# mLSTM layer and two-matrix MLP on one core: the MLP takes 256 tokens at a time, and the first chunk's second matrix is used in float32 before it is divided

## The chip, the cores and the metric

The kernel runs on one NeuronCore of one Trainium2 chip. The metric is the device time of one execution in microseconds (us); several runs are summed up by their median. Engines are called as in the profile: PE (matmul), PEld (the loading of PE's weights), DVE (elementwise and PSUM reads), ACT (activation functions), POOL, and SP, which issues the DMAs here. Every engine works through its own queue in program order and waits on semaphores for the others.

## The reference: what is computed

A gated linear attention over 4 batches, 8 heads and 768 tokens with heads of 40, and behind it a two-matrix MLP over all 3072 tokens, all in float32:

```
for t in range(768):                       # per batch and head
    m_new  = max(f[t] + m, i[t])
    f_s, i_s = exp(f[t] + m - m_new), exp(i[t] - m_new);  m = m_new
    C = f_s * C + i_s * outer(v[t], k[t]);  n = f_s * n + i_s * k[t]
    y[t] = sigmoid(o[t]) * (C @ q[t]) / max(abs(n @ q[t]), 1)
x = y.transpose to (3072, 320)
h = x @ w_in                               # (320, 2048)
out = (h * erf(softplus(h))) @ w_out       # (2048, 320)
```

## The kernel before

**Work.** The 768 tokens of a batch go in six chunks of 128 (`NC = 6`). One *step* is one chunk of one batch: scores of the 8 heads (L454), a decay matrix `dm` times the scores (L463), the product with the values and with the carried state (L482, L486), the state's update (`pk`, L497, L503, L515), the denominators (L522 to L525), the gate (L530, L535), and three transposes into `pt` (L542, L544), from which ACT writes the rounded half `xh` (L551) and DVE the remainder `xl` (L555). Six chunks times four batches make 24 steps.

The MLP follows chunk by chunk, 8 *units* per chunk, 48 in all. The matmuls round their operands (type fp32r), so that each float32 product is made of three: high by high, low by high, high by low. A unit has two `up` tiles (L691, eight matmuls per 128 columns of `w_in`; the last 64 rows of `w_in` are stacked, high over low), which ACT copies to `hb` (L699). ACT then makes softplus (L703) and erf (L708), each for a batch of units, since each needs another function table (L769); DVE multiplies (L713), rounds to `gh` (L717) and subtracts to `gl` (L721). The `down` matmuls take `gh` with `woh` (L740), `gh` with `wol` (L741) and `gl` with `woh` (L738), 320 columns each, into four PSUM tiles `po0` to `po3`, one per batch. ACT copies them to `o`, and a DMA writes them out. In chunk 0 a unit is 256 tokens by 512 columns of `w_in` (L691 streams 256 columns); from chunk 1 on it is all 512 tokens by 256 columns (L691 streams 512).

**Weights.** Both matrices come as 64-bit words and are decoded on the chip in `decode`: DVE shifts (L564), ACT rescales (L569), DVE merges twice (L574, L576). Then ACT writes the high half (L581) and DVE the low half (L586); for every second piece of `w_out` the low half is made on PE by the identity instead (L593, L594, and ACT L598). There are 10 pieces of `w_in` (512 columns) and 16 of `w_out` (320 columns).

**Order.** All operations are first handed to a planner, class `Plan`, with a cost, the tiles that they read and write, and a due time. It walks through time with one server per engine and takes, among the operations that are ready and whose tiles are free, the one that is due first. The instructions are issued in exactly that order. `SLOTS` says how many tiles of each name there are (3 of `raw`, 4 of `hb` and of `n0`, 2 of `qk`, `kvo` and `dm`), `nominal(g) + LAG` gives the due time of unit g's down matmuls, `STEP` that of the attention steps.

Of the kernel before, what the change touches and what calls it, by code (L numbers as in the profile page):

```python
# [18 lines left out]
L = 128  # L19
# [6 lines left out]
T = B * L  # L26
# [7 lines left out]
class Plan:  # L34
# [4 lines left out]
    SWITCH = 1.5  # L39
# [3 lines left out]
    def __init__(self, slots):  # L43
        self.slots = dict(slots)
# [63 lines left out]
    def run(self, switch):  # L108
# [6 lines left out]
        slots = dict(self.slots)  # L115
# [18 lines left out]
        while count < n:  # L134
# [5 lines left out]
            while ends and ends[0][0] <= now + 1e-9:  # L140
                t, i = heapq.heappop(ends)
                o = self.ops[i]
                for k in o.tiles:
                    using[k] -= 1
                    if using[k] == 0:
                        slots[self.tag[k]] += 1
                for s in o.succ:
                    q = self.ops[s]
                    lat = 0.0 if q.eng == o.eng and o.eng != 'SP' else self.LAT[o.eng]
                    ready[s] = max(ready[s], t + lat)  # L150
                    left[s] -= 1
                    if left[s] == 0:
                        cand[q.eng].append(q)
                        wake(max(ready[s], now))
            for e in ('PE', 'DVE', 'ACT', 'POOL', 'SP'):
# [34 lines left out]
                for k in o.new:  # L190
                    slots[self.tag[k]] -= 1
                    if self.tag[k] in self.INORDER:
# [20 lines left out]
        self.span = max(o.end for o in self.ops)  # L213
        return [fn for _, fn in order]
# [3 lines left out]
BATCHES = [[2, 2, 2, 2]] * 6  # L218
SLOTS = dict(gt=1, m=2, x=2, aT=2, qk=2, kvo=2, dm=2, eT=1, vg=1, den=2, xh=2, xl=2, o=2,
             raw=3, hb=4, n0=4, gh=2, gl=2, pa=2, h=2, gd=2, **{f'po{b}': 1 for b in range(B)})  # L220
START = 30.0
LAG = 22.0
XAT = ((2, 3), (0, 2))
STEP = ((4.5, 5.5, 6.5, 7.5), (1.0, 2.0, 5.0, 6.0))
SLOW = 9.0


def nominal(g):
    return START + (SLOW * g if g < 8 else SLOW * 8 + EVERY * (g - 8))
EVERY = 8.6  # L230
# [3 lines left out]
def tile_mlstm_moe(  # L234
# [15 lines left out]
    plan = Plan(SLOTS)  # L250
    t = {}

    def new(tag, shape, key, dtype=F32):
        pool = ps if tag in ('pa', 'h') or tag[:2] == 'po' else sb
        t[key] = pool.tile(shape, dtype, name=tag, tag=tag, bufs=SLOTS[tag])
        return t[key]

    def op(eng, cost, r=(), w=(), tile_=None, **kw):
# [5 lines left out]
    step_due = [None]  # L264

    def dma(kb, r=(), w=(), tile_=None, **kw):
# [4 lines left out]
    nident = cp.tile([128, 128], F32R, name="nident")  # L271
    m0 = cp.tile([128, 1], F32, name="m0")
    zero = cp.tile([128, 1], F32, name="zero")
    state = [cp.tile([128, NPR, 2 * V1], F32, name=f"state{b}") for b in range(B)]
# [3 lines left out]
    wol = cp.tile([128, NFF, DM], F32R, name="wol")  # L278
# [5 lines left out]
    @op('POOL', 2.0, w=[('ident', 0)])  # L284
    def _():
        make_identity(nc, ident)

    @op('ACT', 0.2, r=[('ident', 0)], w=[('nident', 0)])
    def _():
        nc.scalar.activation(nident, ident, AF.Copy, scale=-1.0)  # L290

    @op('POOL', 0.2, w=[('m0', 0)])
# [4 lines left out]
    for b in range(B):  # L297
        @op('POOL', 0.5, w=[('st', b)])
        def _(b=b):
            nc.gpsimd.memset(state[b], 0.0)  # L300
# [3 lines left out]
    soft, erfs = {}, {}  # L304
    exps[0] = [plan.phase('X')] * 2
    for c in range(NC):
        g = 8 * c
        for i, n in enumerate(BATCHES[c]):
            if c + 1 < NC and i in XAT[c > 0]:
                exps[c + 1][XAT[c > 0].index(i)] = plan.phase('X')  # L310
            s = plan.phase('S')
            e = plan.phase('G')
            for j in range(n):
                soft[g + j], erfs[g + j] = s, e
            g += n


    def gate_chunk(c):
# [6 lines left out]
        @op('DVE', 0.35, r=[(('gt', c), 0), *prev], w=[(('m', c), 0)], tile_=('m', ('m', c)))  # L325
# [7 lines left out]
        @op('DVE', 0.9, r=[(('gt', c), 0), (('m', c), 0), ('m0', 0)], w=[(('x', c), 0)], tile_=('x', ('x', c)))  # L333
# [17 lines left out]
        def _():  # L351
            p = new('pa', [128, 512], ('pA', c))
            new('aT', [128, 128], ('aT', c))
            nc.tensor.transpose(p[:, 0:128], t['x', c][:, 0], ident)

        @op('ACT', 0.2, r=[(('pA', c), 0)], w=[(('aT', c), 0)])
# [7 lines left out]
        for b in range(B):  # L364
            @dma(8, r=[(('x', c), 0), (('x', c), 2)], w=[(('gd', c), b)], tile_=('gd', ('gd', c)) if b == 0 else None)
# [6 lines left out]
    def attention(s):  # L372
        c, b = divmod(s, B)
        last = c == NC - 1
        K = lambda n, i=0: ((n, s), i)
        A = lambda n: t[n, s]
        st = state[b]
        due = nominal(8 * (c - 1) + STEP[c > 1][b]) if c else START - 30 + 6 * b
        ph = exps[c][b // 2]

        @dma(416, w=[K('qk', 'q'), K('qk', 'k')], tile_=('qk', ('qk', s)))
        def _():
            nc.sync.dma_start(new('qk', [128, 2, NPR, L], ('qk', s))[0:QR], qk[c, b])

        @dma(484, w=[K('kvo', 'k'), K('kvo', 'v'), K('kvo', 'o')], tile_=('kvo', ('kvo', s)))
        def _():
            nc.sync.dma_start(new('kvo', [128, KVO], ('kvo', s)), kvo[c, b])

        kn = lambda: A('kvo')[:, 0:DM].rearrange("p (h d) -> p h d", d=D)
        v1 = lambda: A('kvo')[:, DM:KV].rearrange("p (h d) -> p h d", d=V1)  # L390
        th = lambda: A('kvo')[:, KV:KVO]
        dm = lambda: A('dm').rearrange("p (n j) t -> p j n t", j=2)
        bias = lambda: t['aT', c][:, 32 * b:32 * b + H].unsqueeze(2)

        if c == 0:
            for i in range(2):
                @op('PE', 1.9, r=[(('x', c), 0), ('ident', 0)], w=[K(f'pb{i}')], tile_=('h', (f'pb{i}', s)), kind='a')
                def _(i=i):
                    p = new('h', [128, 512], (f'pb{i}', s)).rearrange("p (h t) -> p h t", t=L)
                    for h in range(4):  # L400
                        k = 32 * b + 4 * i + h
# [3 lines left out]

                @op('ACT', 0.5, r=[K(f'pb{i}')], w=[K('dm', 0), K('dm', 1)], phase=ph,
                    tile_=('dm', ('dm', s)) if i == 0 else None)
                def _(i=i):
                    if i == 0:
                        new('dm', [128, H, L], ('dm', s))  # L410
                    nc.scalar.activation(A('dm')[:, 4 * i:4 * i + 4], A(f'pb{i}').rearrange("p (h t) -> p h t", t=L), AF.Exp)
        else:
            @dma(512, r=[(('gd', c), b)], w=[K('dm', 'e0'), K('dm', 'e1')], tile_=('dm', ('dm', s)))
            def _():
                nc.sync.dma_start(new('dm', [128, H, L], ('dm', s)).rearrange("p h t -> p (h t)"),
                                  t['gd', c][0, b].rearrange("h t -> (h t)").partition_broadcast(128))

            @dma(208, r=[(('gd', c), b)], w=[K('eT')], tile_=('eT', ('eT', s)))
            def _():
# [415 lines left out]
```

## Time and profile before

| | |
|---|---|
| median of 3 runs (lowest to highest) | 534.78 us (531.88 to 536.58) |
| the profiled execution's own time | 533.4 us |
| its span in the trace | 531.7 us, so 1.7 us lie around it |
| mean granted TensorE clock | 0.956 |
| PE, PEld | 483.9 us (91%), 418.4 us (79%) |
| DVE, ACT, POOL | 354.6 us (67%), 318.1 us (60%), 51.8 us (10%) |
| DMA | 54.16 MB, mean 102 GB/s |

[...] What a matmul costs in a stream is read from the distance of two starts, or from the chain of work, which counts each piece once.

### The profile page before, as it was taken

Reading aid. Unit: us, or ns where it says so; the run is one execution under the profiler, and the core shown is the slowest. Engines: PE = TensorE matmul, PEld = TensorE weight load, DVE = VectorE, ACT = ScalarE, POOL = GpSimd, SP = SyncE. Lnnn points to the kernel's source line nnn. Section 1 sums busy time; section 2 is a strip of 40 time slices with the busy share of each in tenths; the row PEclk is TensorE's granted clock in tenths of the full one; section 3 lists DMA queues with packets and bytes.
Section 4 is the critical chain, followed back from the end, with each engine's and each line's share of the span. In section 5 each row is a group of like instructions: output and inputs, shape, how many; then the busy total and the mean of one; then the engine's idle time right before and its main releaser. Section 6 shows DMA issues by size and latency. Waiting matters only on the chain.

```text
span 531.7 us, 13705 instructions
## 1 busy us (share of the span) xinstructions
PE 483.9 (91%) x5933; PEld 418.4 (79%) x5933; DVE 354.6 (67%) x607; ACT 318.1 (60%) x430; POOL 51.8 (10%) x60
## 2 busy tenths in 40 slices
PE   5967885877969999999999999999999999999995
PEld 5955784866848788888798897888888888888985
DVE  1788688989885658866956667777388457434334
ACT  2545587484474747477487287386476573766651
POOL 2210003001011003003021021030030030000000
PEclk9976698799799999999999999999999999999999
DMA  8558514636451430451623324504405400000001
GB/s 212 177 161 249 172 56 143 197 101 199 144 147 63 120 127 10 119 127 51 204 52 94 108 55 128 175 4 127 126 1 182 120 18 1 2 32 19 1 0 49
DMA packets 28171, 54.16 MB, mean 102 GB/s; under 512 B 2896, under 2 KB 16144, under 8 KB 28112
## 3 DMA queue, kind: packets, MB, share of 16 engines
q1 hardware_dynamic: 28112, 53.30, 34.4%
q8 instruction: 46, 0.75, 0.6%
q14 instruction: 13, 0.11, 0.1%
HBM read 48.14 MB, written 4.10 MB: 98 GB/s over the span
## 4 chain that ended last, share of the span: by engine, by line
PE 62%; DVE 23%; ACT 9%; issue 4%; DMA 2%; SPq 0%; DVEq 0%; ACTq 0%
PE h L691 30%; PE po L740 7%; PE po L738 7%; PE po L741 7%; DVE n L713 4%; PE pa L454 3%; DVE gl L721 3%; ACT L769 2%; PE pa L482 2%; DVE gh L717 2%; DVE raw L576 2%; PE pa L486 2%; DVE raw L574 2%; ACT n L703 2%; ACT n L708 2%
## 5 line engine op out<-in xcount | busy, mean ns | idle before, releaser
L699 ACT ACTIVATE hb<-h 128x512 f32<-128x512 f32 x96 | 56.5, 598 | 132.4 <-PE h L691 132.2
L691 PE MATMUL h<-xh,wh 128*128 128x512 f32 (+1 forms) x336 | 128.0, 383 | 2.2 <-ACT xh L551 1.2
L691 PE MATMUL h<-xl,wh 128*128 128x512 f32 (+1 forms) x336 | 125.3, 376 | 1.3 <-DVE xl L555 1.2
L740 PE MATMUL po<-woh,gh 128*128 128x320 f32 x384 | 118.2, 318 | 8.6 <-DVE gh L717 8.6
L741 PE MATMUL po<-wol,gh 128*128 128x320 f32 x384 | 116.0, 312 | 0.7 <-DVE wol L586 0.5
L713 DVE TENSOR_TENSOR n<-n,hb 128x1024 f32<-128x1024 f32 x48 | 58.6, 1220 | 82.5 <-ACT n L708 82.5
L436 POOL TENSOR_SCALAR_AFFINE_SELECT dm<-dm 128x512 f32<-128x512 f32 x48 | 49.8, 1066 | 378.5 <-ACT dm L431 278.8
L691 PE MATMUL h<-xh,wl 128*128 128x512 f32 (+1 forms) x224 | 84.1, 375 | 0.4 <-DVE wl L586 0.4
L740 PEld LDWEIGHTS po<-woh,gh 128*128 128x128 f32 x384 | 72.9, 190 | 13.6 <-DVE gh L717 6.0
L738 PE MATMUL po<-woh,gl 128*128 128x320 f32 x384 | 79.6, 314 | 0.0
L691 PEld LDWEIGHTS h<-xh,wh 128*128 128x128 f32 x336 | 66.9, 199 | 15.6 <-issue 2.9
L769 ACT ACT_TABLE_LOAD x59 | 75.7, 1283 | 1.8 <-PEq L823 0.8
L691 PEld LDWEIGHTS h<-xl,wh 128*128 128x128 f32 x336 | 66.9, 199 | 10.5 <-DVE xl L555 1.9
L741 PEld LDWEIGHTS po<-wol,gh 128*128 128x128 f32 x384 | 73.0, 190 | 2.5 <-DVE wol L586 1.1
L738 PEld LDWEIGHTS po<-woh,gl 128*128 128x128 f32 x384 | 61.7, 189 | 2.2 <-issue 1.9
L721 DVE TENSOR_TENSOR gl<-n,gh 128x1024 fp32r<-128x1024 f32 x48 | 60.8, 1267 | 3.1
L703 ACT ACTIVATE n<-hb 128x1024 f32<-128x1024 f32 x48 | 50.9, 1059 | 1.5
L691 PEld LDWEIGHTS h<-xh,wl 128*128 128x128 f32 x224 | 44.8, 200 | 8.0 <-DVE wl L586 0.7
L708 ACT ACTIVATE n<-n 128x1024 f32<-128x1024 f32 x48 | 49.1, 1053 | 0.2
L463 DVE TENSOR_TENSOR dm<-pa,dm 128x512 f32<-128x512 f32 x48 | 30.8, 683 | 12.1 <-PE pa L454 12.1
L717 DVE CAST gh<-n 128x1024 fp32r<-128x1024 f32 x48 | 35.8, 746 | 2.7
L482 PE MATMUL pa<-state,qk 104*32 104x82 f32 x640 | 25.5, 242 | 6.4 <-DVE qk L469 5.1
(70 smaller groups left out, 526.9 us busy)
## 6 DMA issues: line engine op xcount, KB each, us to landing
kvo<-in_kvo_dram SPq DMA_DIRECT2D x24, 484.0 KB
dm<-gd SPq DMA_DIRECT2D x20, 512.0 KB
qk<-in_qk_dram SPq DMA_DIRECT2D x24, 416.0 KB
raw<-in_w_out_dram SPq DMA_DIRECT2D x16, 320.0 KB
raw<-in_w_in_dram SPq DMA_DIRECT2D x8, 512.0 KB
out_dram<-o SPq DMA_DIRECT2D x24, 160.0 KB
eT<-gd SPq DMA_DIRECT2D x20, 128.0 KB
eT<-gd SPq DMA_DIRECT2D x20, 80.0 KB
```

The costliest lines, as they stand in the source:

```text
L436: nc.gpsimd.affine_select(out=dm()[:, j], in_=dm()[:, j], pattern=[[0, NPR], [1, L]], compare_op=ALU.is_ge, fill=0.0, base=0, channel_mult ...
L691: nc.tensor.matmul(h[:, n * N:(n + 1) * N], w, m, start=(k == 0), stop=(k == len(ops) - 1))
L699: nc.scalar.activation(G('hb')[:, hs], G(f'h{i}'), AF.Copy)
L703: nc.scalar.activation(new('n0', [128, 1024], ('n0', g)), G('hb'), AF.Softplus)
L708: nc.scalar.activation(n0, n0, AF.Erf)
L713: nc.vector.tensor_tensor(n0, n0, G('hb'), op=ALU.mult)
L717: nc.vector.tensor_copy(new('gh', [128, 1024], ('gh', g), F32R), G('n0'))
L721: nc.vector.tensor_tensor(new('gl', [128, 1024], ('gl', g), F32R), G('n0'), G('gh').bitcast(F32), op=ALU.subtract)
L738: nc.tensor.matmul(po, a[:, ts], woh[:, j], start=False, stop=(j == NFF - 1))
L740: nc.tensor.matmul(po, a[:, ts], woh[:, j], start=(j == 0), stop=False)
L741: nc.tensor.matmul(po, a[:, ts], wol[:, j], start=False, stop=False)
L769: order = plan.run(nc.scalar.preload_act_table_set and (lambda k: nc.scalar.preload_act_table_set(KIND[k])))
```

## The change

**Halves.** Every chunk's MLP now goes in two halves of two batches (`T = 2 * L`, `mlp(g)`: k is the half, q the quarter of the 2048 columns). All `up` matmuls stream 256 columns (L729, 1536 of them instead of 640 with 512 and 256 with 256). `xh` and `xl` are tiles of 256 tokens, and a half's units need the steps of two batches alone. The four tiles `po0` to `po3` become the two banks of one tile `pob`, used by every half in turn; the first chunk's second half borrows a `pa` tile. All `pa` tiles are 1024 wide (two banks).

**First chunk in float32.** Units 0 to 7 skip L717 and L721: their down matmul takes the float32 product itself with the undivided float32 weights `wo` (L779, one instruction of float32 in place of three of fp32r). `decode` writes `wo` directly in its last merge (L625). The division into `woh` (ACT, L698) and `wol` (DVE, L702) comes later, in `split_out`, all 16 on these two engines. The identity products on PE (L593, L594) and their ACT copies are gone.

**Attention.** The state keeps 41 columns per head pair instead of 82, so the state product is 32 small matmuls of 40 rows by 41 columns (L491) instead of 16 of 104 rows by 82. The state update `pk` shares the tile of the head products. Three full transposes (L509) take the place of two and two half ones, after a copy of 64 columns on DVE (L575). The products of scores and decay are one DVE instruction (L525) instead of two. From chunk 2 on the matmuls of two batches stand together (`bundles`).

**Gap filling.** Where the planner's own timetable leaves PE idle for more than 0.9, it puts in matmuls of the identity into an unused corner of `pob` (L826): 31 in all, 13 of them before the first product.

**Slots and dues.** Eight names share 23 tiles of 4 KB (`WIDE`); `raw` may have 6, `hb` and `n0` 5, `qk`, `kvo`, `dm` 3. Costs of the planner's operations and all due times are new.

```diff
-T = B * L
+T = 2 * L
...
-    SWITCH = 1.5
+    SWITCH = 1.35
+    GAP, FILL = 0.9, 0.6
...
+                    if sum(self.tag[k] in self.shared for k in o.new) > total:
+                        continue
...
+        if stay:
+            last = None
+            for o in sorted((o for o in self.ops if o.eng == 'PE'), key=lambda o: o.start):
+                if last is not None and o.start - last.end > self.GAP:
+                    n = int((o.start - last.end) * self.FILL / 0.23)
+                    order.append((last.end, lambda n=n: stay(n)))
+                last = o
...
-SLOTS = dict(gt=1, m=2, x=2, aT=2, qk=2, kvo=2, dm=2, eT=1, vg=1, den=2, xh=2, xl=2, o=2,
-             raw=3, hb=4, n0=4, gh=2, gl=2, pa=2, h=2, gd=2, **{f'po{b}': 1 for b in range(B)})
+SLOTS = dict(gt=1, m=2, x=2, aT=2, qk=3, kvo=3, dm=3, eT=2, vg=2, den=3, xh=2, xl=2, o=2, raw=6, wo=NFF + 1,
+             hb=5, n0=5, gh=2, gl=2, pa=2, h=2, gd=2, po0=1, po1=1)
+WIDE, WIDES = ('qk', 'kvo', 'dm', 'raw', 'hb', 'n0', 'gh', 'gl'), 23
+FIRST_DUE = [23.7, 87.5, 23.0, 49.5, 86.4, 67.7, 62.7, 193.4]
...
+            def full():
+                new('wo', [128, DM], W)
...
+    def split_out(j):
+        W, N = ('wo', j), ('wol', j)
+        @op('ACT', 0.4, r=[(W, 0)], w=[('woh', j)])
+            nc.scalar.activation(woh[:, j], t[W], AF.Copy)
+        @op('DVE', 0.48, r=[(W, 0), ('woh', j)], w=[(N, 0)], tile_=('wo', N))
+            nc.vector.tensor_tensor(new('wo', [128, DM], N, F32R), t[W], woh.bitcast(F32)[:, j], op=ALU.subtract)
...
     def mlp(g):
-        c, q = divmod(g, 8)
+        k, q = divmod(g, 4) if g >= 8 else (g % 2, g // 2)
+        c, half = divmod(k, 2)
...
+        plain = g < PLAIN
+        if not plain:
...
+                        if plain:
+                            nc.tensor.matmul(acc(b), G('n0')[:, ts], t['wo', j], start=(j == 0), stop=(j == NFF - 1))
+                        elif lo:
+                            nc.tensor.matmul(acc(b), G('gl')[:, ts], woh[:, j], start=False, stop=(j == NFF - 1))
+                        else:
+                            nc.tensor.matmul(acc(b), G('gh')[:, ts], woh[:, j], start=(j == 0), stop=False)
+                            nc.tensor.matmul(acc(b), G('gh')[:, ts], t['wol', j], start=False, stop=False)
...
+    def stay(n):
+        for _ in range(n):
+            nc.tensor.matmul(pob[:, 1, 384:512], ident, ident, start=False, stop=False, skip_group_check=True)
```

The order that results, at the places that the prediction speaks of. First DVE's queue where the first two units' products leave it. In the kernel before, `n_585` and `n_814` are the products of units 0 and 1:

```order
L713 TENSOR_TENSOR n_585<-n_585,hb 128x1024
L717 CAST gh<-n_585 128x1024
L721 TENSOR_TENSOR gl<-n_585,gh 128x1024
L713 TENSOR_TENSOR n_814<-n_814,hb 128x1024
L717 CAST gh<-n_814 128x1024
L721 TENSOR_TENSOR gl<-n_814,gh 128x1024
```

In the changed kernel the first two products are `n_765` and `n_823`:

```order
L749 TENSOR_TENSOR n_765<-n_765,hb 128x1024
L612 TENSOR_SCALAR raw<-raw 128x320
L449 TENSOR_TENSOR dm<-dm,aT 128x1024
L612 TENSOR_SCALAR raw<-raw 128x320
L749 TENSOR_TENSOR n_823<-n_823,hb 128x1024
L612 TENSOR_SCALAR raw<-raw 128x320 x2
```

The rounding and the subtraction behind each product have gone; the decoding of `w_out` (L612) and the decay matrix of chunk 1 (L449) stand there now.

Then PE's queue in the first chunk's down matmuls. Before, around the step of chunk 1 and batch 2 (`po_944` and `po_965` are two of the four output tiles):

```order
L740 MATMUL po_965<-woh,gh 128x320
L741 MATMUL po_965<-wol,gh 128x320
L738 MATMUL po_944<-woh,gl 128x320 x4
L454 MATMUL pa<-qk 64x128 x16
L738 MATMUL po_965<-woh,gl 128x320 x4
L593 MATMUL pa<-raw,ident 128x320
L594 MATMUL pa<-woh,nident 128x320
```

In the changed kernel, with the last units of the first chunk (`n_1044`, `n_1084`, `n_1495`) and the transposes of chunk 1's first two batches (L509):

```order
L779 MATMUL pob<-wo,n_1044 128x320 x8
L509 MATMUL pa<-ident,kvo 128x128 x3
L779 MATMUL pa<-wo,n_1084 128x320 x8
L509 MATMUL pa<-ident,kvo 128x128 x3
L779 MATMUL pob<-wo,n_1495 128x320 x8
L479 MATMUL pa<-qk 64x128 x16
```

The twelve fp32r matmuls per batch of a unit have become four in float32, the identity products are gone, and the first half of chunk 1 is through its attention while the first chunk's last units are still to come.

More of the change, by code (lines that the diff above doesn't have):

```diff
@@ L282, in _ @@
         nc.sync.dma_start(cst, consts)
[L284 to L292, printed above, removed]
+    @op('POOL', 0.3, w=[('m0', 0)])
     def _():
@@ L369, in _, with attention @@
                 nc.sync.dma_start(t['gd', c][:, b].rearrange("i h t -> h i t"), t['x', c][32 * b:32 * b + H, 1:3])
-    def attention(s):
-        c, b = divmod(s, B)
+    def attention(c, bs):
         last = c == NC - 1
[L375 to L401, printed above, removed]
@@ L433, in attention @@
-        for j in range(2):
-            @op('POOL', 0.95, w=[K('dm', j)])
-            def _(j=j):
-                nc.gpsimd.affine_select(out=dm()[:, j], in_=dm()[:, j], pattern=[[0, NPR], [1, L]],
-                                        compare_op=ALU.is_ge, fill=0.0, base=0, channel_multiplier=-1)
-        if not last:
-            @op('DVE', 0.42, r=[K('dm', 0), K('dm', 1), K('kvo', 'v')], w=[K('vg')], tile_=('vg', ('vg', s)))
-            def _():
-                vg = new('vg', [128, H, V1], ('vg', s))
-                nc.vector.tensor_tensor(vg, v1(), A('dm')[:, :, L - 1:L].to_broadcast([128, H, V1]), op=ALU.mult)
@@ new lines, in _ @@
+            @op('POOL', 2.1, w=[K('dm', b)])
+            def _(b=b):
+                for i in range(2):
+                    x = A('dm', b)[:, 4 * i:4 * i + 4]
+                    nc.gpsimd.affine_select(out=x, in_=x, pattern=[[0, 4], [1, L]],
+                                            compare_op=ALU.is_ge, fill=0.0, base=0, channel_multiplier=-1)
+            @op('ACT', 0.38, w=[K('kvo', b, 'o')], **(dict(sets='XG') if c else dict(phase=ph)))
+            def _(b=b):
+                nc.scalar.activation(th(b), th(b), AF.Tanh, scale=0.5)
@@ new lines, in attention, with _, scores @@
+            if not last:
+                @op('DVE', 0.55, r=[K('dm', b), K('kvo', b, 'v')], w=[K('vg', b)], tile_=('vg', ('vg', c, b)))
+                def _(b=b):
+                    nc.vector.tensor_tensor(new('vg', [128, H, V1], ('vg', c, b)), v1(b),
+                                            A('dm', b)[:, :, L - 1:L].to_broadcast([128, H, V1]), op=ALU.mult)
+        def scores(b):
+            x = wide(new('pa', [128, 1024], ('S', c, b)))
+            q, k = A('qk', b)[:, 0], A('qk', b)[:, 1]
@@ L550, in _, with turned @@
[L550 to L562 removed]
+        def turned(b):
+            p = new('pa', [128, 1024], ('pt', c, b))
+            for i in range(3):
+                nc.tensor.transpose(p[:, i * L:(i + 1) * L], A('kvo', b)[:, KV + i * 128:KV + (i + 1) * 128], ident)
@@ L563, in _, with decode @@
+    def decode(key, raw, n, full, out, **first):
+        R = key
+        @op('DVE', n / 1020 + 0.005, r=[(R, 0)], w=[(R, 1)])
         def _():
@@ new lines, in tile_mlstm_moe @@
+    gate_chunk(0)
+    for i in range(2):
+        step_due[0] = STEPS[i]
+        attention(0, (2 * i, 2 * i + 1))
+    step_due[0] = None
+    for part in range(4):
+        step_due[0] = WIN[part]
+        for k in range(2):
+            weights_in(part, k)
+        if part % 2 == 0:
+            step_due[0] = WIN[4 + part // 2]
+            weights_tail(part // 2)
+        step_due[0] = WOUT[part]
+        for j in range(4):
+            weights_out(4 * part + j)
+    step_due[0] = None
+    for g in range(8):
+        mlp(g)
```

549 lines of the change are left out of this document (282 added, 267 removed).

## Prediction

> **What bounds the kernel now.** I begin with the slices, since an average over 532 us says little here.
>
> ```profile
> PE   5967885877969999999999999999999999999995
> DVE  1788688989885658866956667777388457434334
> PEclk9976698799799999999999999999999999999999
> ```
>
> A slice is 13.3 us. Up to the twelfth PE has holes and the clock dips, while DVE stands at 8 and 9; from the thirteenth on PE is full and DVE falls off. So there are two stages, and I ask for the busy time of each, with two shorter stretches of the first (columns: stretch, its length, busy time and count of PE, PEld, DVE, ACT, POOL, granted clock, DMA share, GB/s).
>
> ```profile
> 33.94:160.00 126.06, 99.87 (x1367) 86.12 (x1367) 104.83 (x211) 76.74 (x121) 8.41 (x10) 0.84 0.51 151
> 160.00:205.00 45.00, 43.71 (x533) 37.45 (x535) 28.76 (x45) 28.21 (x37) 5.77 (x5) 0.99 0.29 91
> 205.00:513.50 308.50, 305.54 (x3571) 262.48 (x3568) 195.00 (x299) 192.66 (x237) 30.51 (x26) 1.00 0.27 76
> 40.00:80.00 40.00, 33.33 (x396) 28.94 (x396) 31.01 (x68) 25.94 (x44) 0.00 (x0) 0.79 0.54 160
> 120.00:160.00 40.00, 31.24 (x459) 26.10 (x460) 35.65 (x71) 20.86 (x32) 3.14 (x4) 0.88 0.54 162
> ```
>
> From 33.94, where the first up tile starts, to 160 DVE works 104.83 of 126.06 us, 83%. PE's 99.87 there are stretched by a clock of 0.84. From 205 to 513.5 PE works 305.54 of 308.50 at full clock, and DVE 63%. **DVE sets the first stage, PE the second.** The boundary is the first chunk's last product; the third row below is it. The others give what the second stage is made of (chain of work: start, length, what).
>
> ```profile
> 33.94 3.52 PE h L691 x16
> 162.75 1.17 PE po L738 x8
> 158.76 1.22 DVE L713 TENSOR_TENSOR n<-n,hb 128x1024 f32<-128x1024 f32 x1
> 204.91 1.03 PE pa L454 x32
> 429.50 1.03 PE pa L454 x32
> 466.21 3.76 PE h L691 x16
> 473.49 3.76 PE h L691 x16
> 509.86 3.76 PE h L691 x16
> ```
>
> A down matmul costs 1.17 / 8 = 0.147 us. Without attention a unit takes 473.49 - 466.21 = 7.28 us. The scores at 204.91 and at 429.50 stand at the same place of chunks three apart, so a chunk with attention takes 224.6 / 3 = 74.9; less 8 units (58.2) it leaves 16.7 for four steps, 4.2 us a step, with all waits and changes between small and large matmuls in it. Behind the last up tile (509.86 + 3.76) are 72 down matmuls, 10.6 us; the span ends at 531.7, so 7.5 us are a tail that is not matmul work.
>
> **The change, first stage.** I count DVE's queue in both orders from the second `xl` (behind which the first up tile starts) to the point from which PE is fed. Before, that is the eighth product, at 160. In the changed order I take the last `xl` of chunk 1, which stands behind all eight products and the first unit's `gh`: everything that chunk 1 needs of DVE but its own products is then done.
>
> ```profile
> L721 DVE TENSOR_TENSOR gl<-n,gh 128x1024 fp32r<-128x1024 f32 x48 | 60.8, 1267 | 3.1
> L713 DVE TENSOR_TENSOR n<-n,hb 128x1024 f32<-128x1024 f32 x48 | 58.6, 1220 | 82.5 <-ACT n L708 82.5
> L717 DVE CAST gh<-n 128x1024 fp32r<-128x1024 f32 x48 | 35.8, 746 | 2.7
> L463 DVE TENSOR_TENSOR dm<-pa,dm 128x512 f32<-128x512 f32 x48 | 30.8, 683 | 12.1 <-PE pa L454 12.1
> L427 DVE TENSOR_TENSOR dm<-dm,aT 128x1024 f32<-128x1024 f32 x20 | 24.4, 1220 | 6.2 <-DMA dm<-gd 6.2
> L443 DVE TENSOR_TENSOR vg<-kvo,dm 128x328 f32<-128x328 f32 x20 | 12.5, 625 | 9.0 <-POOL dm L436 7.6 <-ACT n L703 1.2
> L574 DVE SCALAR_TENSOR_TENSOR raw<-raw 128x512 int32<-128x512 int32 x10 | 7.5, 754 | 0.1
> L576 DVE SCALAR_TENSOR_TENSOR raw<-raw 128x512 int32<-128x512 int32 x10 | 7.2, 725 | 0.3
> L586 DVE TENSOR_TENSOR wl<-raw,wh 128x512 fp32r<-128x512 f32 x8 | 5.2, 683 | 0.0
> L564 DVE TENSOR_SCALAR raw<-raw 128x512 int32<-128x512 int32 x10 | 5.1, 508 | 3.1 <-DMA raw<-in_w_in_dram 3.1
> L586 DVE TENSOR_TENSOR wol<-raw,woh 128x320 fp32r<-128x320 f32 x8 | 3.9, 482 | 0.0
> ```
>
> Removed: 7 `gh` and 7 `gl`, 7 x (0.746 + 1.267) = 14.1. Of the 7 pieces of `w_in` decoded there, one full merge and two shifts now lie earlier, 0.754 + 0.725 + 0.683 + 2 x 0.508 = 3.2. The score products are 5 full ones instead of 12 halves, 12 x 0.683 - 5 x 1.28 = 1.8 (a full one I estimate as two halves less one start). Added: chunk 1's first product, `gh` and `gl`, 3.2; 13 divisions instead of 8, 2.4; two decay additions, 2.4; one `vg`, 0.6; one more block for the gates, six short copies and less for the narrower state, together about 2.4 (an estimate from rows like L443). Net 19.1 - 11.0 = 8.1, so DVE has 104.8 - 8.1 = 96.7 us of work in the stage.
>
> How long that takes depends on DVE's idle time, 21.2 us before. A part of it waits for weights (who waited for whom in 40 to 160: total, times, longest):
>
> ```profile
> DVE raw L564 <- DMA raw<-in_w_in_dram: 2.8, 1, 2.8
> DVE raw L564 <- DMA raw<-in_w_out_dram: 1.3, 2, 1.0
> ```
>
> With six tiles of `raw` instead of three these 4.1 go: 104.83 / 121.96 is 86%. I take 86%, so 96.7 / 0.86 = 112.4 and the stage ends at 33.9 + 112.4 = **146.3**. The ends: DVE never idle, 130.6; as in the worst stretch of the table (31.01 of 40, 77.5%), 158.7. The start at 33.9 I leave: in the new order 2.2 us more of DVE work lie ahead of the second `xl`, but decoding can fill DVE's wait at the beginning.
>
> Queues that are touched too: the divisions move ACT's copies into `woh` to chunk 1's beginning, and ACT is 61% busy in the stage (76.74 of 126.06). SP issues the weights earlier, at 51% DMA share. Both I cost at nothing; if ACT's cover went, the 16 divisions at 0.49 would show, 7.8 us.
>
> **Second stage.** Behind the transposes that feed that last `xl`, PE's new order still holds 960 fp32r down matmuls, 4 in float32, 1168 up matmuls and 16 steps. The prices:
>
> ```profile
> 11.41 0.39 PE L404 MATMUL h<-ident,x 128*128 128x128 f32 x2
> 11.63 0.39 PE L403 MATMUL h<-x,ident 128*128 128x128 f32 x2
> 103.18 0.28 PE L691 MATMUL h<-xl,wh 128*128 128x256 f32 x1
> 106.71 0.28 PE L691 MATMUL h<-xl,wh 128*128 128x256 f32 x1
> 210.32 0.14 PE pa L482 x8
> 210.47 0.15 PE pa L486 x16
> 448.86 0.38 PE L542 MATMUL pa<-ident,kvo 128*128 128x128 f32 x2
> 449.17 0.44 PE L544 MATMUL pa<-ident,kvo 128*64 128x128 f32 x4
> 449.54 0.50 PE L691 MATMUL h<-xh,wh 128*128 128x512 f32 x1
> ```
>
> *Up:* chunk 0 streams 256 columns already. Thirty starts lie between 103.18 and 106.71, 0.118 us each; with 512 columns it is 3.76 / 16 = 0.235. **The halves cost PE nothing**, 1168 x 0.118 = 137.8. *Down:* 960 x 0.147 = 141.1. *Float32:* 128 columns take 11.63 - 11.41 = 0.22 us, so 320 take 0.55; the first chunk's 64 cost 35 us for 192 x 0.147 = 28 before, but all but 4 (2.2 us) lie in the first stage, where DVE is the bound. *Steps:* the state product (4 groups of about 0.15) loses at most half its columns, 0 to 0.3 us; three whole transposes at 0.155 replace 0.68 us, 0.2 saved; joining two batches halves the changes of matmul shape, for which I put 0.1. So 4.2 becomes 3.7, with 3.4 and 4.2 as ends: 16 x 3.7 = 59.2. *Tail:* 7.5, since the last unit's chain is the same. *New waits:* each half reuses the two banks of `pob`, so at ten seams PE waits for ACT's copy; at nine of them up matmuls of 1.9 us or more stand between and hide it, one is bare, 1 to 3 us, inside the step's range. *Gap filling:* 31 x 0.22 = 6.8 us, put where PE was planned idle; uncovered, at most that.
>
> **The sum:** 146.3 + 137.8 + 141.1 + 2.2 + 59.2 + 7.5 = 494.1 us of span. The profiled execution of before took 533.4 with a span of 531.7, and the median shown is 534.8; 1.7 + 1.4 on top gives **497 us**.
>
> [...] The row first: in the stage up to 160 the clock is 0.84, so 32% of 126 us, 40 us, ran at half speed. [...] If the filling matmuls held it and PE set the stage, PE would win back up to 20 us; DVE sets it, so my sum takes nothing. [...]
>
> **Rivals.**
> - *Tight first stage* (chance 0.17). DVE hardly idles, PE stays warm and steps cost 3.4: 130.6 to 138 + 288.6 + 54.4 + 3.1 gives 477 to 484. For it: more tiles. Against: DVE's queue is in order and even the best stretch was 35.65 of 40.
> - *Two full engines wait for each other* (0.18). Before, PE had slack while DVE was busy. In the new order PE's work up to 146 (368 up, 60 float32 downs, 8 steps, the decay matmuls of chunk 0) comes to about 120 us, so a late DVE result is no longer absorbed. At 77.5% and steps of 4.2: 158.7 + 288.6 + 67.2 + 3.1 = 518.
> - *It does not do what it says* (0.05): the divisions only move DVE's and ACT's work to chunk 1, whose units wait; with 8 us for them on top of the last case 526 to 535.
> - *Slower: the weight loads come out from under the matmuls* (0.04).
>
> ```profile
> L691 PEld LDWEIGHTS h<-xl,wh 128*128 128x128 f32 x336 | 66.9, 199 | 10.5 <-DVE xl L555 1.9
> ```
>
> Twice as many loads of 199 ns stand against matmuls of 0.118. If each matmul waited for its load, 1280 of them would take 0.199 instead of 0.118, 104 us more, 600 us. It turns the result from a spacing of 0.118 + 37 / 1280 = 0.147 on. Against it: the thirty starts above were not load-bound. [...]
>
> **How the numbers follow.** The forecast, 487 to 508, has 0.56; the rivals have 0.17, 0.18, 0.05 and 0.04. The range goes from the tight case to the coupled one, 477 to 518. A measurement of this kernel can tell about 1% (529 to 540) from no change. Forecast, tight and coupled case are faster, 0.91; half of the fourth lies within 1%, and I give that 0.05; slower 0.04.
>
> **What would show it.** Right: the eighth product near 117 to 120, the last `xl` of chunk 1 near 146, DVE at 86% until then; up matmuls 0.118 apart; a clock over 0.95 from 34 to 150; 7.3 us per unit at the end. Wrong: PE idle behind 150 with DVE as releaser, up spacing over 0.13, or waits of PE for `o` at the seams of halves.

## Result and the profile after

The changed kernel takes 550.6 us (548.9 to 555.5) against 533.9 for the kernel before in the same comparison: **1.032 times as long, with a 95% interval of 1.024 to 1.041.** The forecast was 497, the range 477 to 518. The profiled execution took 549.4 us, its span is 547.7. Of two kernels below, `nofill` and `state_pad`, one run each was over 1.5% slower than the fastest; the medians leave it out, but the profile of `state_pad` is that run's (552.7 us against a median of 545.7).

The slices first (PE's busy tenths, and the granted clock):

```profile
PE   8978899698997989889959978995999699989996
PEclk9979999989897989979969996998799979999999
```

The picture is turned round. Before, PE and its clock had their holes in the first twelve slices; now those are fuller, and the holes stand further back, where PE used to be full. The stretches (length, then busy time and count of PE, PEld, DVE, ACT, POOL, clock, DMA share, GB/s) and two rows of DVE's timeline:

```profile
33.90:117.00 83.10, 74.19 (x999) 63.08 (x999) 71.40 (x157) 65.90 (x106) 6.85 (x8) 0.96 0.64 192
160.00:205.00 45.00, 38.82 (x903) 37.15 (x902) 29.30 (x60) 28.09 (x36) 4.51 (x6) 0.89 0.42 120
205.00:513.50 308.50, 278.01 (x3906) 270.91 (x3906) 171.80 (x268) 163.52 (x205) 20.61 (x22) 0.92 0.22 64
```

```profile
118.52 1.22 DVE L749 TENSOR_TENSOR n<-n,hb 128x1024 f32<-128x1024 f32 x1
154.60 0.55 DVE L604 TENSOR_TENSOR xl<-pa,xh 128x384 fp32r<-128x384 f32 x1
```

The first chunk's last product starts at 118.5 instead of 158.8, and the clock before it is 0.96 instead of 0.84: the first stage gained 40 us. From 205 to 513.5 PE works 278.0 of 308.5 us where it worked 305.5, at a clock of 0.92 where it had 1.00. Who made PE wait there (150 to 500; total, times, longest):

```profile
PE pa L491 <- issue: 18.6, 5, 6.3
PE pa L495 <- issue: 9.0, 3, 5.0
PE pa L503 <- issue: 8.0, 5, 2.1
```

35.6 us, none of it on another engine: "issue" is time in which PE waited for nothing that the profile shows. All of it stands in the *head products*, as the small matmuls of a step are called from here on: the product with the state (L491), the product with the values (L495) and the state's update (L503). One place, two batches joined (PE's timeline: start, length, matmul records, idle time before; a float32 matmul leaves two records):

```profile
272.95 0.78 PE L491 MATMUL pa<-state,qk 40*32 40x41 f32 x64
273.67 0.82 PE L495 MATMUL pa<-kvo,dm 128*32 128x41 f32 x64
274.30 0.49 PE L503 MATMUL pa<-vg,kvo 128*32 128x41 f32 x32
274.71 0.35 PE L491 MATMUL pa<-state,qk 40*32 40x41 f32 x23
280.15 0.76 PE L491 MATMUL pa<-state,qk 40*32 40x41 f32 x41 [5.09 <-issue]
280.83 1.32 PE L495 MATMUL pa<-kvo,dm 128*32 128x41 f32 x64
281.93 0.63 PE L503 MATMUL pa<-vg,kvo 128*32 128x41 f32 x22
283.93 0.43 PE L503 MATMUL pa<-vg,kvo 128*8 128x41 f32 x10 [1.37 <-issue]
```

PE stops in the middle of one and the same line, where no semaphore stands. From the first stop to the second it executes 41 + 64 + 22 = 127 matmul records, each with its weight load: 254 instructions, one record short of 256. The page's rows on instructions tell what that number is:

```profile
PE 489.6 (89%) x7117; PEld 462.2 (84%) x7117; DVE 338.1 (62%) x599; ACT 312.5 (57%) x419; POOL 41.8 (8%) x60
q8 instruction: 56, 0.92, 0.7%
```

56 packets with 0.92 MB are 16,384 bytes each, and 2 x 7117 / 56 is 254 instructions a packet. **PE stops where one packet of instructions ends and the next has not come.** The places bear it out: counted in PE's matmul records from the start of the trace, the 13 stops behind 150 stand at 2256, 2383, 2892, 3401, 3528, 4038, 4165, 4675, 4803, 5312, 5439, 6075 and 6712, each 127 or 128 records from the last or about a whole multiple of that, and at each PE goes on 1.2 to 1.6 us after a packet has landed. The kernel before had 46 packets and no wait of PE by issue behind 150. (A batch's head products, 80 float32 matmuls here, are 160 records or, with the loads, 320 instructions. A *burst* is a run of such small matmuls with no large one in between; a joined one has 640 instructions, the longest of the kernel before had 256.)

The longest stops stand where data is under way, which no run here varies by itself; the page counts packets and data as shares of the same 16 DMA engines (0.7% and 33.1%). The traffic around the stop of 5.09 us, from 272 to 288 in slices of 0.4 us (a lone 41 is one packet):

```profile
GB/s 297 297 195 225 266 317 297 225 287 225 236 195 236 318 113 0 0 0 0 0 0 0 0 41 0 0 0 0 0 0 0 0 41 0 0 0 0 0 3 161
```

The packet that ends this stop starts at 277.55, among the last of the data, 4.1 us after PE has entered the packet before it. At the three longest stops, 5.0, 5.1 and 6.3 us, the DMA engines were 92 to 97% busy from PE's entering until the packet started, and 6.7 to 8.0 us passed from entering to going on. At the eight stops where that share was at most 27% it was 3.5 to 4.0 us; the other two had 87 and 99%, and 3.8 and 4.6 us.

### The profile page after: what moved, and what is told of

The parts are those of the page before. It is cut to its first block, busy times and chain, and to the rows that moved or that the text cites. A ratio compares the mean times of both kernels' runs of the same rounds, so it can differ in the third digit from the quotient of the medians.

```text
span 547.7 us, 15952 instructions
## 1 busy us (share of the span) xinstructions
PE 489.6 (89%) x7117; PEld 462.2 (84%) x7117; DVE 338.1 (62%) x599; ACT 312.5 (57%) x419; POOL 41.8 (8%) x60
## 3 DMA queue, kind: packets, MB, share of 16 engines
q1 hardware_dynamic: 28112, 53.30, 33.1%
## 4 chain that ended last, share of the span: by engine, by line
PE 85%; issue 9%; ACT 3%; DVE 2%; POOL 0%; ACTq 0%; POOLq 0%
PE h L729 33%; PE pob L783 9%; PE pob L784 9%; PE pob L781 9%; PE pa L495 4%; PE pa L479 4%; PE pob L779 3%; PE pa L779 3%; PE pa L491 3%; PE pa L503 2%; PE pa L509 2%; PE pob L826 1%; PE pa L427 1%; PE pa L428 1%; ACT L828 1%
## 5 line engine op out<-in xcount | busy, mean ns | idle before, releaser
L729 PE MATMUL h<-xh,wh 128*128 128x256 f32 x576 | 163.2, 292 | 1.7 <-ACT hb L737 1.7
L729 PE MATMUL h<-xl,wh 128*128 128x256 f32 x576 | 160.1, 287 | 0.0
L729 PEld LDWEIGHTS h<-xh,wh 128*128 128x128 f32 x576 | 111.7, 194 | 9.1 <-issue 6.4
L729 PEld LDWEIGHTS h<-xl,wh 128*128 128x128 f32 x576 | 111.6, 194 | 0.4 <-DVE xl L604 0.2
L729 PE MATMUL h<-xh,wl 128*128 128x256 f32 x384 | 110.2, 287 | 0.0
L783 PE MATMUL pob<-woh,gh 128*128 128x320 f32 x320 | 101.4, 327 | 1.3 <-ACT o L789 1.1
L784 PE MATMUL pob<-wo,gh 128*128 128x320 f32 x320 | 99.1, 321 | 0.0
L729 PEld LDWEIGHTS h<-xh,wl 128*128 128x128 f32 x384 | 74.5, 194 | 0.0
L783 PEld LDWEIGHTS pob<-woh,gh 128*128 128x128 f32 x320 | 63.9, 200 | 3.1 <-ACT o L789 1.6
L784 PEld LDWEIGHTS pob<-wo,gh 128*128 128x128 f32 x320 | 64.0, 200 | 0.1
L781 PE MATMUL pob<-woh,gl 128*128 128x320 f32 x320 | 61.0, 318 | 0.0
L781 PEld LDWEIGHTS pob<-woh,gl 128*128 128x128 f32 x320 | 51.1, 195 | 0.4 <-issue 0.2
L495 PE MATMUL pa<-kvo,dm 128*32 128x41 f32 x1536 | 23.8, 219 | 16.6 <-issue 16.6
L495 PEld LDWEIGHTS pa<-kvo,dm 128*32 128x32 f32 x1536 | 20.0, 123 | 21.3 <-issue 20.1
```

The lines of the kernel that those rows point to most:

```text
L495: nc.tensor.matmul(y[ts, j, p], w[:, j, p, ts], v[:, 2 * p + j], start=(c == 0), stop=(c == 0 or p == NPR - 1))
L729: nc.tensor.matmul(h[:, n * T:(n + 1) * T], w, m, start=(s == 0), stop=(s == len(ops) - 1))
L781: nc.tensor.matmul(acc(b), G('gl')[:, ts], woh[:, j], start=False, stop=(j == NFF - 1))
L783: nc.tensor.matmul(acc(b), G('gh')[:, ts], woh[:, j], start=(j == 0), stop=False)
L784: nc.tensor.matmul(acc(b), G('gh')[:, ts], t['wol', j], start=False, stop=False)
```

## The experiments

Theory F: bursts of small matmuls outrun the packets of instructions, and the half clock behind each stop comes on top (in the changed kernel from 150 to 500 eight stretches at 0.50, of 3.4 to 10.2 us and 58.0 in all, each of which begins during a stop or at most 1.4 us behind one). The rivals were S (the joined steps wait for tiles or semaphores that the profile does not name), C (the clock itself, by the shape of the matmuls) and G (the filling matmuls stand in the way). "Waits" is the sum of PE's waits released by issue from 150 to 500 in the profiled execution, "clock" the granted one from 160 to 490. Each ratio is to runs of the kernel before in the same round (medians of 533.5 to 534.5).

| kernel | instructions in the longest burst | us | ratio to before (interval) | waits | clock |
|---|---|---|---|---|---|
| before | 256 | 533.9 | 1 | 0 | 1.00 |
| after | 640 | 550.6 | 1.024 to 1.041 | 35.6 | 0.92 |
| `single` | 320 | 536.3 | 1.001 to 1.007 | 26.8 | 0.95 |
| `wide` | 192 | 542.7 | 1.004 to 1.017 | 0 | 0.92 |
| `nofill` | 640 | 541.8 | 1.008 to 1.016 | 29.7 | 0.94 |
| `state` | 512 | 511.2 | 0.949 to 0.960 | 22.6 | 0.97 |
| `state_pad` | 640 | 545.7 | 1.017 to 1.028 | 35.0 | 0.93 |
| `shift` | 640 | 538.8 | 1.005 to 1.017 | 31.6 | 0.93 |
| `shift_block` | 640 | 552.0 | 1.027 to 1.038 | 35.7 | 0.91 |
| `state_single` | 256 | 511.1 | 0.953 to 0.962 | 15.0 | 0.98 |
| `state_pk8` | 448 | 508.6 | 0.949 to 0.956 | 15.5 | 0.98 |
| `state_single_pk8` | 224 | 510.2 | 0.952 to 0.961 | 13.8 | 0.98 |
| `split_pk8` | 192 | 508.3 | 0.947 to 0.957 | 8.4 | 0.98 |
| `state_pk8_s8` | 448 | 512.6 | 0.958 to 0.967 | 19.1 | 0.97 |
| `pk8_shift16` | 448 | 501.2 | 0.933 to 0.942 | 11.0 | 0.98 |
| `pk8_shift32` | 448 | 512.1 | 0.952 to 0.962 | 17.1 | 0.97 |
| `pk8_divided` | 448 | 527.9 | 0.982 to 0.994 | 19.3 | 0.96 |

**Joining, shape, filling.** `single` never joins two batches:

```diff
-BUNDLE, PLAIN = 2, 8
+BUNDLE, PLAIN = NC, 8
```

> The changed kernel, except that the matmuls of two batches never stand together (BUNDLE = NC: each step's scores, head products and transposes are planned by themselves). Theory F (PE runs out of instructions: the instructions come in packets of 16,384 bytes, 256 instructions, about 3.5 us apart at the closest, and a burst of small matmuls uses them up faster): the longest burst falls from 640 instructions to 320, so PE's long idle times released by issue behind 150 us, which sum to about 39 us in the changed kernel (1.6 to 6.6 us each), shrink to under 20 us, none over 4 us, and the time comes to 515 to 530. Theory S (joined steps wait for tiles or semaphores that the profile does not name): also faster, about the same, but then the waits would go whatever the size of the burst. Theory C (the half clock itself is the cause): the clock does not depend on joining, 545 to 555.

`state` takes the state product of the kernel before (and its 82 state columns):

```diff
-                    for j in range(2):
-                        js = slice(64 * j, 64 * j + D)
-                        nc.tensor.matmul(y[ts, j, p], q[js, p, ts], st[js, p], start=(p == 0), stop=False)
+                    nc.tensor.matmul(y[ts, 2 * p:2 * p + 2].rearrange("p h d -> p (h d)"),
+                                     q[0:QR, p, ts], st[0:QR, p], start=True, stop=False)
```

> The changed kernel, two batches joined, with the state product of the kernel before: 16 matmuls of 104 rows by 82 columns per step in place of 32 of 40 by 41. A joined burst is 512 instructions instead of 640. Theory F: two packets instead of two and a half, so the idle times released by issue fall by a quarter to a half, 530 to 542. Theories S and C: 547 to 555.

`wide` takes the full width of the array for the head products (shown: the values), `nofill` leaves the filling matmuls out (`plan.run` without `stay`):

```diff
-                    for ts in quarters:
-                        nc.tensor.matmul(y[ts, j, p], w[:, j, p, ts], v[:, 2 * p + j], start=(c == 0),
+                    nc.tensor.matmul(y[:, j, p], w[:, j, p], v[:, 2 * p + j], start=(c == 0),
```

> The changed kernel with two batches still joined, but the head products with the full width of the array: values, state and state update are 8 matmuls each per step in place of 32, 32 and 16 (128 columns of weights instead of four times 32, 40 instead of 32 and 8). The arithmetic is the same; a joined burst of head products falls from 640 instructions to 192, less than one packet. Theory F: the idle times released by issue nearly go (under 10 us behind 150 us), and the time comes to 500 to 520, less what the wider matmuls cost (between nothing and 1 us a step, 20 us in all). Theories S and C: joining and the clock are as before, so no gain; with the wider matmuls 550 to 570.

> The changed kernel without the matmuls that fill planned gaps (31 in all). Theory F: no part of the loss behind 150 us, so 545 to 553; in the first stage the clock may fall below 0.96. Theory G (the filling matmuls stand in PE's way where the plan's gaps do not exist): 6 to 8 us less, 540 to 545. Theory C (the clock is the cause): without filling it is lower still, 555 or more.

`single` gained 14 us and lost 9 us of waits, less than F had promised (515 to 530 us, under 20 us of waits). `state` gained 39, twice what F had promised, which at this point spoke for the shape as much as for the number. `wide` did what F says of the waits: none is left behind 150. Its time (500 to 520 expected) was a miss, for two reasons that its timeline shows:

```profile
280.19 1.09 PE L490 MATMUL pa<-state,qk 40*128 40x41 f32 x16
281.21 1.98 PE L493 MATMUL pa<-kvo,dm 128*128 128x41 f32 x16
283.12 0.51 PE L500 MATMUL pa<-vg,kvo 128*40 128x41 f32 x16
283.56 1.30 PE L490 MATMUL pa<-state,qk 40*128 40x41 f32 x16
284.79 3.63 PE L493 MATMUL pa<-kvo,dm 128*128 128x41 f32 x16
```

The values take 1.98 us instead of 0.82, and the second batch 3.63 for the same 16 records: by that the clock has halved, although PE never idled there (the clock is 0.92 from 160 to 490; PE's waits from 150 to 500 come to 1.1 us). `nofill` came out nearly 9 us faster, as G said and F had not; but the 31 fillers are 124 instructions, the last at 103 us, and leaving them out moves every packet boundary behind them.

**Number or shape.** `state_pad` is `state` with 16 one-column matmuls per step, so that a joined burst has 640 instructions again:

```diff
+                if c > 0:
+                    for ts in quarters:
+                        nc.tensor.matmul(pob[ts, 1, 384:385], q[0:QR, p, ts], st[0:QR, p, 0:1], start=False, stop=False,
+                                         skip_group_check=True)
```

> The kernel state (511.2 us; two batches joined, state product of 104 rows by 82 columns), in the same order, with 16 more matmuls per step among its head products, of 104 rows and a single column, whose results nothing reads. A joined burst is 640 instructions again, as in the changed kernel, but the state product keeps its shape. Theory F (the number of instructions in a burst decides): waits released by issue and half clock come back, 535 to 552. Theory C (the shape decides: 40 rows by 41 columns let the clock fall, and the waits follow it): only the matmuls' own time comes on top, 20 steps x 32 records x 7 to 15 ns, 5 to 10 us, 516 to 522.

34.5 us came back, with 35.0 us of waits. The added matmuls' own starts add up to 11.5 us behind 120, 4.8 us of stops among them included. And the stops are at the places of the changed kernel: the same 13 record numbers (2256, 2383, 2892 and so on to 6712, three of them off by one), though the state product there has another shape. **The number of instructions decides, not the shape**; C as the cause falls.

**Boundaries.** `shift` and `shift_block` put 32 and 64 small matmuls (half a packet, a whole packet) at the start, where PE has nothing to do. Nothing else differs:

```diff
+        for i in range(32):
+            at = 32 * i % 128
+            nc.tensor.matmul(pob[at:at + 32, 1, 384:425], ident[0:40, at:at + 32], ident[0:40, 0:41],
+                             start=False, stop=False, skip_group_check=True)
```

> The changed kernel, in the same order, with 32 small matmuls (128 instructions, half a packet) more at its very start, where PE has nothing to do yet. They move every boundary between two packets by half a packet against the steps. Theory F: the boundaries fall at other places of the bursts, so the list of PE's waits behind 150 us changes (times and lengths), and the time moves by up to 10 us either way; without the filling matmuls, which moved them by as much, it was 542. Theory C and any other in which the order and the shapes decide: 548 to 553, the same waits at the same matmuls.

> The changed kernel, in the same order, with 64 small matmuls (256 instructions, one whole packet) more at its very start. Every boundary between packets falls where it fell in the changed kernel. Theory F: the changed kernel's time and waits again, 547 to 555, against 538.8 with half a packet. If the 32 matmuls acted in another way (a warmer clock at the start, a later start of PE): 64 act at least as much, 530 to 540.

PE's waits from 150 to 500, first of `shift`, then of `shift_block`:

```profile
PE pa L499 <- issue: 19.8, 6, 5.5
PE pa L495 <- issue: 10.1, 3, 6.2
PE h L733 <- issue: 1.7, 1, 1.7
```

```profile
PE pa L495 <- issue: 19.4, 5, 5.7
PE pa L499 <- issue: 8.8, 3, 6.1
PE pa L507 <- issue: 7.5, 5, 2.4
```

(The lines are four further down than in the changed kernel: 495, 499, 507 are its 491, 495, 503.) Half a packet gave 12 us, a little more than the 10 expected, and another list of waits; a whole packet gave the changed kernel's time and its list again, 5, 3 and 5 waits at the same three lines, and each of the 13 at the same matmul (record numbers 2384, 2511, 3020 and so on, 128 higher throughout). More work at the start, the other explanation, would have acted twice as much. This also takes the ground from G: `nofill` takes out 124 instructions where `shift` adds 128, which puts the boundaries in nearly the same places, and its two main waits are nearly those of `shift` (18.6 us in 5 and 8.6 in 3, at the same two lines).

**The pace itself.** `bursts` is `state_single` with bursts behind its last matmul (run once):

```diff
+        for n in (32, 64, 128, 256):
+            burst(n, 40, 32, 41)
+            calm(128)
```

> The kernel state_single with extra matmuls behind its last one, whose results nothing reads: 256 matmuls of 128 columns (fp32r), then four bursts of 32, 64, 128 and 256 float32 matmuls of 40 rows, 32 columns of weights and 41 columns (four instructions each: 128, 256, 512 and 1024), a burst of 128 of 40 rows, 64 and 128 columns (512 instructions), and a burst of 64 with 128 columns of weights and 41 columns (256 instructions, no packet needed within); 128 calm fp32r matmuls stand behind each. At 17 ns a record (as in the steps) the four take 1.1, 2.2, 4.4 and 8.7 us. Theory F+: the first two take about that (the second up to 3 us more), the third 3 to 6 us more with a gap released by issue, the fourth 14 to 18 us in all with a packet of 16,384 bytes every 3.5 to 4 us; the fifth, at 32 ns a record, 8.2 us with no gap over 1 us; the sixth about 8 us without a gap, and yet half clock in it or right behind. Theory C alone: no gaps in any burst, only a halved clock, the fourth 9 to 17 us. Theory S: no gaps, no other duration than that of the records, since no semaphore stands in them.

PE's timeline of the second, third and fourth burst, and the DMA traffic from 596 to 612 in slices of 0.4 us:

```profile
547.52 1.40 PE L835 MATMUL pob<-ident 40*32 40x41 f32 x128
563.29 1.82 PE L835 MATMUL pob<-ident 40*32 40x41 f32 x172
567.33 1.72 PE L835 MATMUL pob<-ident 40*32 40x41 f32 x84 [2.22 <-issue]
596.48 3.22 PE L835 MATMUL pob<-ident 40*32 40x41 f32 x172
600.37 2.41 PE L835 MATMUL pob<-ident 40*32 40x41 f32 x128 [0.68 <-issue]
603.83 2.41 PE L835 MATMUL pob<-ident 40*32 40x41 f32 x128 [1.05 <-issue]
607.29 1.71 PE L835 MATMUL pob<-ident 40*32 40x41 f32 x84 [1.05 <-issue]
```

```profile
GB/s 0 0 0 0 0 41 0 0 0 0 0 0 0 41 0 0 0 0 0 0 0 0 41 0 0 0 0 0 0 0 0 41 0 0 0 0 0 0 0 0
```

256 instructions passed without a stop; the longer bursts ran 172 records (344 instructions) and then stopped after every 128, with 603.83 - 600.37 = 607.29 - 603.83 = **3.46 us a packet**, and the only traffic is one packet in each period. At full clock 172 records took 1.82 us, so PE wants a packet's worth every 1.4. No semaphore stands in the bursts, so S, which expected no gaps, falls. The third burst took 5.8 us, 1.4 more than the 4.4 reckoned without a stop (3 to 6 more expected), the fourth 12.5, less than the 14 to 18 expected. The fifth and sixth burst tell nothing: the clock stayed at half for the rest of the program, and they took 27.6 us each.

In the changed kernel too the next packet came late: the packets that ended the 13 stops started 0.7 to 5.5 us after PE had entered the packet before, and PE waited 35.6 us.

**Towards a better kernel.** All these start from `state`: never joined (`state_single`), the state update as 8 matmuls of 40 columns (`state_pk8`), both (`state_single_pk8`), both with the update planned by itself (`split_pk8`), and joined with 8 full-width matmuls for the scores (`state_pk8_s8`).

```diff
-                    for d in (slice(0, 32), slice(32, D)):
-                        for j in range(2):
-                            nc.tensor.matmul(pk[64 * j + d.start:64 * j + d.stop, p], k[:, 2 * p + j, d], vg[:, 2 * p + j],
-                                             start=True, stop=True)
+                    for j in range(2):
+                        nc.tensor.matmul(pk[64 * j:64 * j + D, p], k[:, 2 * p + j], vg[:, 2 * p + j], start=True, stop=True)
```

> The changed kernel with both edits: the state product of the kernel before (16 matmuls of 104 rows by 82 columns) and batches never joined. With state alone 511.2 us, with joining alone undone 536.3. Theory F+ (two losses: PE waits for instruction packets where a burst is longer than the packets at hand, and the clock halves where PE streams few columns or waits): a step's burst is 256 instructions, one packet, so the idle times released by issue behind 150 us fall from 24 us to under 12, half clock there from 17 us to under 10, 490 to 503 us. Theory S (joining hurts by tiles, and the state product by its own duration, with nothing in common): gains add up, 511 - 14 = 497, but with waits released by issue as in state, over 20 us. If joining pays where the bursts are short: 511 or more.

> The kernel state (two batches joined, state product of before) with the state update as 8 matmuls of 128 by 40 per step in place of 16 of 32 and 8: a joined burst falls from 512 to 448 instructions. PE's own time for it is the same (16 records took 0.51 us in wide, 32 records 0.48). Theory F+: fewer packets needed within a burst, 5 to 10 us less than state, 501 to 507. Theory C alone (only the share of the array that works counts): no change, 508 to 514.

> All three edits on the changed kernel: state product of before, batches never joined, state update as 8 matmuls. A step's burst is 224 instructions. Theory F+: waits released by issue under 8 us behind 150, 488 to 500, at or a little below state_single. Theory S: as state_single within 2 us.

> State product of before, batches never joined, state update as 8 matmuls and planned by itself again (as in the kernel before), so that other matmuls may stand between it and the head products: bursts of 64, 192 and 32 instructions. Theory F: waits released by issue behind 150 us fall under 6 us (state_single_pk8: about 17), 495 to 505. If the bursts are no longer what costs: 508 to 514 as state_single_pk8.

> State product of before, batches joined, state update as 8 matmuls, and the scores as 8 matmuls per step with the full width (40 rows, 128 columns of weights, 128 columns) in place of 16 with 64. A joined burst of scores falls from 128 to 64 instructions; the head products stay at 448. Theory F: a little below state_pk8 (508.6), 502 to 508. If the full width costs PE time as it did with 41 columns: 510 to 520.

Waits fell further, the time hardly. `state_pk8` came out 2.6 us below `state`, in the range of C (508 to 514) and just above that of F+ (501 to 507); the difference is too small to tell them apart. For the three unjoined kernels the expectations were too low (490 to 503, 488 to 500, 495 to 505), and their waits (15.0, 13.8, 8.4) fell less than expected (under 12, 8, 6). It seems that unjoined steps cost elsewhere what they save: their chain of work lies on DVE for 13 to 17%, that of `state` and `state_pk8` for 6 and 8%. No run tests this. The scores in full width did not pay. The boundaries were then moved under `state_pk8` by a quarter and half a packet (16 and 32 matmuls at the start, as in `shift`):

> The kernel state_pk8 (508.6 us) with 16 small matmuls (64 instructions, a quarter of a packet) more at the start. Theory F: the two long waits at chunks 3 and 5 (5.3 and 5.1 us, each with two windows of half clock behind it) move or go, and others may come: 500 to 514, with another list of waits. Otherwise: 507 to 510 with the same list.

> The kernel state_pk8 with 32 small matmuls (128 instructions, half a packet) more at the start. Theory F: 500 to 514, with a list of waits that differs from both others. Otherwise: 507 to 510 with the same list.

501.2 and 512.1 against 508.6: 11 us between kernels that differ by a few idle matmuls at the start. `pk8_shift16` beats both kernels, 0.938 times the time before. Its clock in 40 slices:

```profile
PEclk9989999999999999999979999999999999999999
```

**The first stage.** `pk8_divided` divides the weights ahead of the first chunk (`PLAIN = 0`, `split_out` before `mlp(0)`) in `state_pk8`:

> The kernel state_pk8 with the first chunk's second matrix divided before use, as in every other chunk (PLAIN = 0, and split_out ahead of the first chunk's units). By the prediction's first stage: 8 gh and 8 gl come back ahead of the first chunk's end (8 x 2.0 = 16 us of DVE, 14 of them before the eighth product) and the 16 divisions at 0.49 move ahead too (7.8), so the eighth product comes 20 to 28 us later than the 116.3 of state_pk8, and the end 5 to 20 us later, 513 to 528, since chunk 1 gets DVE's time back. If the undivided weights bring nothing: 505 to 512. The packet boundaries move too, which is worth up to 10 us either way, so the product's time counts for more than the end.

The eighth product (DVE's timeline), first in `state_pk8`, then divided:

```profile
116.30 1.22 DVE L746 TENSOR_TENSOR n<-n,hb 128x1024 f32<-128x1024 f32 x1
```

```profile
140.22 1.21 DVE L746 TENSOR_TENSOR n<-n,hb 128x1024 f32<-128x1024 f32 x1
```

23.9 us later, and 19.3 at the end (where the boundaries have moved too, with 19.3 us of waits instead of 15.5): up to the eighth product the undivided first chunk is worth what the prediction's count of DVE's queue made of it.

## Why the prediction was wrong, step by step

- *First stage: right up to the eighth product.* It was to come at 117 to 120 and came at 118.5, with DVE at 86% (71.40 / 83.10) and the clock at 0.96. How much of that clock the filling matmuls hold is not shown: without them (`nofill`) it was 0.92 from 33.9 to 120 instead of 0.96, but the packet boundaries had moved too. The last `xl` of chunk 1 was 8.3 us late (154.6 instead of 146.3), with DVE at 83% until then. Three stops of PE by issue lie ahead of it, 1.9, 3.0 and 2.5 us; in `pk8_shift16`, which has a single one of 0.8 there, it came at 143.3.
- *Prices of matmuls: right.* Up matmuls stand 0.12 us apart where nothing disturbs them, with weight loads of 0.194 us each (L729), so no load came out from under them; the rival on loads had no ground. The seams at `o` cost 1.1 us.
- *Steps: wrong.* This is the step that failed. I priced the state product by its columns ("loses at most half its columns") and joining by the changes of shape ("I put 0.1"), and counted no instructions. The new form doubles the matmuls, 16 to 32, and joining puts 640 instructions into a burst that wants 3.5 us (two batches of 274.71 - 272.95), while a packet of 256 took 3.46 in `bursts`. The term that I left at nothing is the stops: 16 steps at 3.7 came out as 5.7 each, 90.5 us, and 35.6 of these are stops. Without them 54.9 are left, below the 59.2 of the forecast.

Where the second stage went, in us, from the starts of PE's matmuls (each counted up to the next start, stops included):

| | forecast | after | `pk8_shift16` |
|---|---|---|---|
| last `xl` of chunk 1 | 146.3 | 154.6 | 143.3 |
| 16 steps | 59.2 | 90.5 | 53.7 |
| up matmuls | 137.8 | 146.0 | 143.2 |
| down matmuls | 143.3 | 152.3 | 152.9 |
| tail | 7.5 | 4.3 | 4.3 |
| span | 494.1 | 547.7 | 497.4 |

Of the 53.6 missing, 31.3 stand in the steps, 8.3 ahead of the stage, 17.2 in up and down matmuls, about 14 of it by half clock behind the stops (down matmuls 0.27 apart instead of 0.147 at 285.5 to 286.9, where the clock is 0.50); the tail was 3.2 shorter, though by this count the kernel before has one of 4.9, not 7.5. In the last column, with fewer instructions and luckier boundaries, the steps cost 3.4 us each and the forecast's sum nearly comes true, partly by luck: 15.0 us too much in up and down matmuls stand against 11.7 too little in the rest.

- *Rivals: none was it.* I had PE waiting for DVE, for loads and for `o`; the stops had no partner on any engine. The profile before does not show the loss: behind 150 PE waits for no issue. Its weight loads do, as in this row for the state product:

```profile
PEld pa L482 <- issue: 12.6, 20, 4.2
```

But the longest, 4.2 us at 94.9, stands where PE itself waits 4.0 us for DVE's `qk`, and the common ones, 0.4 us, pass under running matmuls. What could have been read beforehand is the page's instruction row: 46 packets for 2 x 5933 matmul and load records, 258 a packet, against 640 instructions in a joined burst.

## What to carry to other kernels

Count instructions as well as cycles. A float32 matmul was four of them here, and small matmuls that ran through a packet of 256 in under 3.5 us could stop PE at its end, whoever had data ready: from entering a packet to going on 3.5 to 4.0 us passed at stops with the DMA engines at most 27% busy, and up to 8.0 with 92 to 97%. So cutting one matmul into several small ones was not free. Fewer and larger ones (`wide`: no stop, though at a clock of 0.92) and the state update planned apart from the head products (`split_pk8`, 8.4 us of waits instead of the 13.8 of `state_single_pk8`) left less of it. And when an edit moves such a kernel by 2%, shift the boundaries by half a packet and by a whole one before its mechanism is believed: half a packet alone was worth 12 us here.

## What the hardware showed that I had not expected

- A whole packet of idle instructions at the start reproduces the time (552.0 to 550.6), half a packet does not (538.8).
- The clock fell without any idle PE: in `wide` there was no wait by issue from 150 to 500, and the clock was 0.92 from 160 to 490. Why is not settled; ahead of the row of 3.63 us lie 4.6 us (280.19 to 284.79) of matmuls that stream 41 columns.
- In `bursts` the clock stayed at half from the third burst to the end: each of the four blocks of 128 matmuls of 128 columns from 568.98 on took 27.57 us, where the two before took 14.51. What would have brought it back was not tried.
- In `bursts` one packet lay ahead of PE, not more. In the third and the fourth burst PE entered a new packet after 44 records (the stops, counted back by 128, give the place) and stopped 128 later, at its end: 44 + 128 = 172.
- Bursts of 192 to 256 instructions still stopped now and then, by up to 4.4 us. In `state_single_pk8` and `split_pk8`, at all seven stops behind 150, the DMA engines were 81 to 100% busy from PE's entering a packet to the start of the next. Why the kernel before, with bursts of 256, has no such stop stays open; its boundaries were not moved.
